# No token columns zeroed, a drain of GpSimd ahead of the last stores, other homes for a tile and two banks, and weight splits and choosing tied to later steps

## The chip, the cores and the metric

The kernel runs on one core of one Trainium2 chip. The metric is device time in microseconds. Three runs of the kernel before took 411.88, 405.08 and 408.65 us; their median is 408.65.

## The reference

Two layers follow each other. The first is a linear attention with a decay per channel, over B=4 batches, H=8 heads, S=768 steps and D=48 channels. The second is a mixture of experts over the N = 3072 tokens that come out, with DM = 384 channels, E = 8 experts, F = 1024 hidden units and room for 768 tokens in each expert.

```python
f = 1.0 / (1.0 + np.exp(-f_logit))
for t in range(S):
    state = f[:, :, t, :, None] * state + np.einsum('bhd,bhe->bhde', k[:, :, t], v[:, :, t])
    y[:, :, t] = np.einsum('bhd,bhde->bhe', q[:, :, t], state)
x = y.transpose(0, 2, 1, 3).reshape(B * S, H * D)

logits = x @ w_gate
expert_idx = np.argmax(logits, axis=1)
gate_w = softmax(logits)[np.arange(N), expert_idx]
# disp[e] holds the tokens of expert e in their order, at most 768 of them
h = np.maximum(np.einsum('ecd,edf->ecf', disp, w1), 0.0)
y = np.einsum('ecf,efd->ecd', h, w2)
out[i] = gate_w[i] * y[expert_idx[i], pos[i]]      # of the tokens that had room
```

## The kernel before, in words

**Attention.** The 3072 steps of all batches are cut into NT = 24 chunks of 128. A chunk is worked on over several slots of a loop that runs from slot -4 to slot 24 and is written out in order for all engines. Slot n finishes the output of chunk n-1 (`y_out`, ScalarE), pads queries and keys of chunk n+3 (POOL), transposes those of chunk n+2 on TensorE (PE, L343) and multiplies them by the decay's running products on DVE into kT and qT (L388, the products from two scans at L363 and L377), makes the scores of chunk n+1 (PE L399, evicted by ACT L405, masked by POOL L407), and then, for chunk n itself, the part from the carried state (L440), the keys' transposes (L424), the state's update by keys and values (L451) and the values (L481).

**Loads of attention.** SP issues them one after another, each some chunks ahead: `load("v", n + 3)` and `load("kq", n + 6)` in slot n, six buffers for v (ld_v) and three for kq (L195 is kq's load). In slots 1 and 3 SP also zeroes 256 rows of `disp` each (`zero_disp`), and in slots 2 to 5 the token column of 128 rows for each of seven experts (`zero_tokens`, L324). `disp` is the table in memory to which the tokens are sorted by expert, 393 numbers a row: 384 of x, eight logits and the token's number. A row that isn't filled is to hold zero as token, so that its output is dropped. Both read a tile `zero` of zeros (L314), which lies in the pool `apool`, whose memory later tiles reuse.

**Routing.** The rows of a chunk (PE L502) get their logits and are copied to a buffer. Groups of chunks (6, 6, 3, 3, 3, 1, 1, 1) are then routed together: `choose` (DVE, L533 to L540) makes the one-hot choice r_oh from the logits, for a single chunk `choose_one` (its last operation is L552); `rank` counts on PE how many earlier tokens went to each expert (L581, L582, L585, L588); `place` (DVE, L558 to L570) makes row numbers `ri`; and POOL scatters the rows into `disp` by an indirect DMA (L297), one per chunk, 24 in all. A group is chosen in the slot after its last chunk's rows and ranked in the slot after that; for groups that end in the last six chunks both happen in one slot.

**Weights.** Each weight matrix is split into a high and a low part of a narrower type (L131 on ACT for the high one, L140 on DVE or POOL for the low one), and each product is three matmuls: high by high, high by low, low by high. w1 comes in three raw pieces, w2 in four. Expert 0's pieces are loaded and split during attention, in the slots of `PIECE_LOAD` and `PIECE_SPLIT`.

**The experts.** The first 256 tokens of expert 0 are job 0. The first layer of that job runs inside the last slots of attention, by the table `EARLY`: `early_pe(ft)` is the product of hidden block ft (L662, nine matmuls), `early_out(ft)` its eviction into hh (ACT, L668) and hl (DVE, L669). Then attention's accumulators in PSUM, the pools psF and psY (two banks each), are closed and psM (four banks) takes their place. Job 0's second layer (L881) starts; in its middle `order_experts` sorts the seven other experts by their numbers of tokens, and `fill_rows` (three indirect stores of `zero` on POOL) clears the rows of each that its job's size takes in beyond its tokens. Job 1 is expert 0's remaining 224 tokens, and the seven others follow with sizes 480, 440, 424, 408, 396, 384 and 368. Each job loads its rows (`load_rows`), splits and transposes them (`prep`, L1023), computes its gate from the logits in the row (`gates`, L854 is its first difference from the maximum), runs the first layer (`ffn1`, eight hidden blocks of nine matmuls each) and the second, either by rows (`ffn2_rows`, L881, eviction L885) or by channels (`ffn2`, L1049, eviction yT L1054, transposed back at L1065). The output rows go to memory by indirect stores of POOL, 30 in all. For jobs from the third on, the next expert's seven pieces are loaded and split while the present job runs (`load_weights`), through three raw buffers; w1's low parts are made by DVE, w2's by POOL.

**The order.** Attention is written out by hand for all engines, job 0's second layer for PE alone. Everything else is ordered by the scheduler of the language, which runs the program on its own model of durations. `tc.issue_after(ins)` holds an instruction back behind another in that order.

## Time and profile before

| what | value |
|---|---|
| median of three runs | 408.65 us |
| profiled execution, its own time | 409.31 us |
| its span | 407.6 us |
| mean granted clock of TensorE | 0.984 |
| PE busy | 380.5 us, 93% |
| DVE busy | 214.4 us, 53% |
| ACT busy | 208.5 us, 51% |
| POOL busy | 174.6 us, 43% |
| mean DMA rate | 149 GB/s |

Attention takes roughly the first 155 us of the span, job 0's second layer the next few, and the jobs up to 398 us; the rest is the last stores and the program's end. A row of the chain of waits gives the instruction's start in us, its length, the engine or queue, the line with its operation, and in brackets how long the engine had been idle before it and what ended that. SPq, ACTq and POOLq are the engines' own queues with their register, issuing and drain instructions, which do not count as busy. L1285 is the end of the program, where each engine drains.

### The profile page before, as it was taken

How to read it: one execution, taken by the hardware profiler on the slowest of the kernel's cores; microseconds unless marked ns; L12 is line 12 of the kernel's file. 1: busy time of each engine (PE TensorE's matmuls, PEld its weight loads, DVE VectorE, ACT ScalarE, POOL GpSimd, SP SyncE). 2: the span in 40 equal slices, each digit the busy share in tenths (PEclk: the TensorE clock that was granted, in tenths of full speed). 3: DMA queues.
4: the chain of work that ended last, by engine and by line, in shares of the span. 5: the costliest groups of instructions: out<-in, count | busy, mean ns of one | idle time of the engine just before them, and what ended most of it. 6: DMA issues, size and time to landing. Idle time of an engine off the chain costs nothing.

```text
span 407.6 us, 10048 instructions
## 1 busy us (share of the span) xinstructions
PE 380.5 (93%) x3941; PEld 351.3 (86%) x3941; DVE 214.4 (53%) x502; ACT 208.5 (51%) x449; POOL 174.6 (43%) x233
## 2 busy tenths in 40 slices
PE   7699999989899898979999999999999999999990
PEld 7588888877788787979879989999999999999990
DVE  4987897858898654555635262253153262231300
ACT  3467677757677751255546453563563564432210
POOL 7444446757668431408163804424424415421010
PEclk9999999989999998999999999999999999999996
DMA  9999989999994221557676744425525323001010
GB/s 164 185 167 195 192 148 259 239 191 252 251 231 121 80 81 47 200 183 222 241 235 224 242 139 151 168 86 166 170 92 168 124 96 100 39 16 52 0 42 18
DMA packets 86957, 60.91 MB, mean 149 GB/s; under 512 B 69303, under 2 KB 81461, under 8 KB 86900
## 3 DMA queue, kind: packets, MB, share of 16 engines
q1 hardware_dynamic: 82852, 50.05, 51.5%
q0 software_dynamic: 3520, 9.92, 6.7%
q8 instruction: 33, 0.54, 0.6%
q10 hardware_dynamic: 528, 0.20, 0.2%
q14 instruction: 24, 0.20, 0.2%
HBM read 49.42 MB, written 11.44 MB: 149 GB/s over the span
## 4 chain that ended last, share of the span: by engine, by line
PE 53%; issue 15%; DVE 10%; DMA 10%; SPq 3%; ACT 3%; POOL 3%; POOLq 0%; ACTq 0%; DVEq 0%
PE psM L1049 14%; PE psA L662 7%; PE psM L662 7%; DMA ld_v<-in_v_dram 5%; PE psM L881 5%; PE psT L502 4%; DVE Rq L377 4%; PE psA L399 3%; DMA raw<-in_moe_w_dram 3%; SPq L195 2%; POOL out_dram L297 2%; PE psT L1022 2%; PE psT L424 2%; PE psY L440 2%; PE psF L662 2%
## 5 line engine op out<-in xcount | busy, mean ns | idle before, releaser
L140 POOL TENSOR_TENSOR w2l<-raw,w2h 128x768 fp32r<-128x768 f32 x28 | 51.4, 1844 | 78.8 <-ACT w2h L131 66.2
L297 POOL DMA_INDIRECT out_dram<-yo,g_ti x30 | 29.4, 981 | 74.1 <-ACT yo L885 43.5
L669 DVE SCALAR_TENSOR_TENSOR hl<-psA,hh 128x224 fp32r<-128x224 f32 (+7 forms) x32 | 17.9, 563 | 60.6 <-ACT hh L668 60.6
L131 ACT ACTIVATE w2h<-raw 128x768 fp32r<-128x768 f32 x32 | 27.1, 846 | 28.9 <-PE psM L1049 15.4
L407 POOL TENSOR_SCALAR_AFFINE_SELECT AT<-AT 128x512 f32<-128x512 f32 x48 | 29.3, 634 | 28.1 <-ACT AT L405 28.1
L881 PE MATMUL psM<-w2h,hh 128*128 128x384 f32 (+2 forms) x112 | 38.7, 348 | 1.6 <-DVE g_m L854 0.9
L881 PE MATMUL psM<-w2h,hl 128*128 128x384 f32 (+2 forms) x112 | 38.2, 344 | 0.2 <-DVE hl L669 0.2
L881 PE MATMUL psM<-w2l,hh 128*128 128x384 f32 (+2 forms) x112 | 38.2, 344 | 0.0
L1049 PE MATMUL psM<-hh,w2h 128*128 128x440 f32 (+3 forms) x96 | 34.3, 357 | 0.0
L405 ACT ACTIVATE AT<-psA 128x512 f32<-128x512 f32 x48 | 26.0, 594 | 16.0 <-PE psA L399 16.0
L1049 PE MATMUL psM<-hh,w2l 128*128 128x440 f32 (+3 forms) x96 | 33.9, 353 | 0.0
L1049 PE MATMUL psM<-hl,w2h 128*128 128x440 f32 (+3 forms) x96 | 33.8, 352 | 0.0
L669 DVE SCALAR_TENSOR_TENSOR hl<-psM,hh 128x224 fp32r<-128x224 f32 (+7 forms) x32 | 17.8, 563 | 28.3 <-ACT hh L668 28.3
L297 POOL DMA_INDIRECT disp<-rows,ri x24 | 25.6, 1066 | 16.0 <-DVE hl L669 5.2
L668 ACT ACTIVATE hh<-psA 128x224 fp32r<-128x224 f32 (+7 forms) x32 | 15.8, 498 | 30.7 <-PE psA L662 25.5
L363 DVE TENSOR_TENSOR_SCAN Suf<-psF,direv 112x511 f32<-112x511 f32 x24 | 29.1, 1211 | 4.4 <-PE psF L343 4.4
L382 POOL COPY kqp<-ld_kq 128x768 f32<-128x768 f32 x24 | 19.9, 830 | 24.2 <-DMA ld_kq<-in_q_dram 19.3
L662 PE MATMUL psM<-xh,w1h 128*128 128x480 f32 (+6 forms) x84 | 29.8, 355 | 0.0
L662 PE MATMUL psM<-xl,w1h 128*128 128x480 f32 (+6 forms) x84 | 29.7, 354 | 0.0
L140 DVE TENSOR_TENSOR w1l<-raw,w1h 128x1024 fp32r<-128x1024 f32 x21 | 24.8, 1222 | 9.1 <-ACT w1h L131 8.8
L399 PE MATMUL psA<-qT,kT 48*128 48x128 f32 x384 | 29.0, 280 | 0.4 <-DVE r_sel L558 0.2
L662 PE MATMUL psA<-xh,w1h 128*128 128x480 f32 (+6 forms) x84 | 29.4, 350 | 0.0
(223 smaller groups left out, 976.4 us busy)
## 6 DMA issues: line engine op xcount, KB each, us to landing
raw<-in_moe_w_dram SPq DMA_DIRECT2D x24, 512.0 KB, 7.2
raw<-in_moe_w_dram SPq DMA_DIRECT2D x32, 384.0 KB, 3.8
ld_kq<-in_k_dram SPq DMA_DIRECT2D x24, 192.0 KB, 6.6
ld_kq<-in_q_dram SPq DMA_DIRECT2D x24, 192.0 KB, 5.6
ld_v<-in_v_dram SPq DMA_DIRECT2D x24, 192.0 KB
ld_f<-in_f_logit_dram SPq DMA_DIRECT2D x11, 384.0 KB, 6.4
xg<-disp SPq DMA_DIRECT2D x6, 589.5 KB, 5.3
xg<-disp SPq DMA_DIRECT2D x3, 393.0 KB, 3.1
```

The costliest lines, as they stand in the source:

```text
L131: nc.scalar.activation(hi, raw, AF.Copy)
L140: engine.tensor_tensor(lo[cs], raw[cs], hi[cs].bitcast(F32), op=ALU.subtract)
L297: ins = nc.gpsimd.indirect_dma_start(out=dst, out_offset=bass.IndirectOffsetOnAxis(ap=idx, axis=0), in_=rows, in_offset=None, bounds_check ...
L363: nc.vector.tensor_tensor_scan(out=_view(Suf[:R], m - 1, [[-1, m]]), data0=_view(F, m, [[-1, m]]), data1=_view(direv[:R], m - 1, [[-1, m]] ...
L382: nc.gpsimd.tensor_copy(kqp[n % 2][:, :, :, :D], loaded("kq", n).rearrange("t h j d -> t j h d"))
L399: nc.tensor.matmul(pas[s][:, p], kTs[n][r, p], qTs[n][r, p], start=True, stop=True)
L405: nc.scalar.activation(AT[:, s], pas[s], AF.Copy)
L407: nc.gpsimd.affine_select(AT[:, s], AT[:, s], pattern=[[0, NP], [1, C]], compare_op=ALU.is_ge, fill=0.0, base=0, channel_multiplier=-1)
L662: nc.tensor.matmul(ph[:, :T], a[:, c, fs], x[:, c, :T], start=(n == 0), stop=(n == 3 * DT - 1))
L669: nc.vector.scalar_tensor_tensor(out=hl[:, :T], in0=ph[:, :T], scalar=0.0, in1=hh[:, :T].bitcast(F32), op0=ALU.max, op1=ALU.subtract)
L881: nc.tensor.matmul(py[:n], x[:, ks], a[:, ft], start=(ft == 0 and m == 0), stop=(ft == FT - 1 and m == 2))
L1049: nc.tensor.matmul(pys[c][:, :T], a[:, ft, cs], x[:, :T], start=(ft == 0 and n == 0), stop=(ft == FT - 1 and n == 2))
```

## The change

Eight edits are made together.

- `zero_tokens` and its four stores are gone. In `gates` the row number made from the token is taken to be at least zero (`tensor_scalar_max`), one more DVE operation in each of the nine gate calculations. The rows up to each job's size are still cleared by `fill_rows` as before.
- The tile `zero` lies in the pool `const`, which is kept to the end of the program.
- The pool psY is made ahead of psF, so that psM's first two banks are those that were psY's.
- The last block of the early job, `early_pe(7)`, moves behind the last chunk's rows.
- Where a group of several chunks ends before the last six chunks, `choose` waits for the next slot and stands there behind `kq_in`, that is behind the next kT and qT. Four groups are concerned.
- The low parts of expert 0's w2 pieces (DVE) move behind the routing of their slot.
- `load_weights` loads and splits only w1's three pieces. Each of w2's four pieces has its load and split called behind one of the last four hidden blocks of the present job, and the split held behind that block's hh. The first sorted job's own weights are still loaded as before.
- `gpsimd.drain()` is issued behind the last output store of the job before the last, ahead of the last job's three stores.

```diff
@@ -79,8 +79,8 @@
     psT = ctx.enter_context(tc.tile_pool(name="psT", bufs=2, space=PSUM))
     psA = ctx.enter_context(tc.tile_pool(name="psA", bufs=2, space=PSUM))
     pctx = ExitStack()
+    psY = pctx.enter_context(tc.tile_pool(name="psY", bufs=2, space=PSUM))
     psF = pctx.enter_context(tc.tile_pool(name="psF", bufs=2, space=PSUM))
-    psY = pctx.enter_context(tc.tile_pool(name="psY", bufs=2, space=PSUM))
 
 
     ident = const.tile([P, P], F32, name="ident")
@@ -128,7 +128,7 @@
 
     def split_high(piece):
         raw, hi, lo = piece
-        nc.scalar.activation(hi, raw, AF.Copy)
+        return nc.scalar.activation(hi, raw, AF.Copy)
 
     def split_low(piece, engine, parts=1):
         raw, hi, lo = piece
@@ -144,8 +144,13 @@
         split_low(piece, engine)
 
     def load_weights(wt, e, pool):
-        for n in range(DT + FT // 2):
-            split_piece(weight_piece(wt, e, pool, n), nc.vector if n < DT else nc.gpsimd)
+        for n in range(DT):
+            split_piece(weight_piece(wt, e, pool, n), nc.vector)
+
+    def load_later(wt, e, pool, n, ins):
+        piece = weight_piece(wt, e, pool, n)
+        with tc.issue_after(ins):
+            split_piece(piece, nc.gpsimd)
 
     wsets = [weight_tiles(w0pool)]
     xg0 = w0pool.tile([P, T_FIRST[0] // P, W], F32, name="xg0")
@@ -309,7 +314,7 @@
         return ins.ins
 
 
-    zero = apool.tile([P, W], F32, name="zero")
+    zero = const.tile([P, W], F32, name="zero")
     pace = {}
     nc.vector.memset(zero, 0.0)
 
@@ -317,12 +322,6 @@
         ins = nc.sync.dma_start(
             disp[v * RPE : v * RPE + 2 * P, :].rearrange("(a p) w -> p a w", p=P),
             zero.unsqueeze(1).broadcast_to([P, 2, W]),
-        )
-        after(ins, pace["ins"], "behind the first loads")
-
-    def zero_tokens(a):
-        ins = nc.sync.dma_start(
-            dispv[1:NE, a * P : (a + 1) * P, W - 1 :].rearrange("v p o -> p v o"), zero[:, :NS].unsqueeze(2)
         )
         after(ins, pace["ins"], "behind the first loads")
 
@@ -646,7 +645,8 @@
         (NT - 1, 1): ((early_out, 3), (early_pe, 4)),
         (NT - 1, 2): ((early_out, 4), (early_pe, 5)),
         (NT, 0): ((early_out, 5), (early_pe, 6)),
-        (NT, 1): ((early_out, 6), (early_pe, 7)),
+        (NT, 1): ((early_out, 6),),
+        (NT, 2): ((early_pe, 7),),
     }
 
     def early_job(n, at):
@@ -665,13 +665,13 @@
     def hidden_out(ph, T, ft, pool, size):
         hh = pool.tile([P, size], F32R, name=f"hh{ft}")
         hl = pool.tile([P, size], F32R, name=f"hl{ft}")
-        nc.scalar.activation(hh[:, :T], ph[:, :T], AF.Relu)
+        ins = nc.scalar.activation(hh[:, :T], ph[:, :T], AF.Relu).ins
         nc.vector.scalar_tensor_tensor(
             out=hl[:, :T], in0=ph[:, :T], scalar=0.0, in1=hh[:, :T].bitcast(F32), op0=ALU.max, op1=ALU.subtract
         )
-        return hh, hl
-
-    pieces, checks, chosen, split_at = {}, [], {}, {"n": None}
+        return hh, hl, ins
+
+    pieces, checks, chosen, split_at, full = {}, [], {}, {"n": None}, []
     slots = range(-4, NT + 1)
     ends = {g + m - 1: (g, m) for g, m in GROUPS}
 
@@ -703,8 +703,6 @@
                 load("f", 4)
         if n in (1, 3):
             zero_disp(0 if n == 1 else NE)
-        if 2 <= n < 6:
-            zero_tokens(n - 2)
         if n in PIECE_LOAD:
             k = PIECE_LOAD.index(n)
             pieces[k] = weight_piece(wsets[0], 0, raw0, k)
@@ -729,6 +727,9 @@
             kq_pad(n + 3)
         if kqn:
             kq_in(n + 2)
+        while full:
+            g, m = full.pop()
+            chosen[g] = choose(rows_of[g // RT][:, g % RT : g % RT + m], m, abuf), m
         if n == -2:
             keep_busy(7)
         if n % 2 and fn and n not in (-3, 1):
@@ -779,12 +780,12 @@
             queue.extend(range(g, g + m))
             if g + m == SPLIT:
                 split_at["n"] = n + 1
-        for k in pieces:
-            if PIECE_SPLIT[k] == n:
-                split_low(pieces[k], nc.vector)
         if prev and done and not tail:
             g, m = done
-            chosen[g] = choose(rows_of[g // RT][:, g % RT : g % RT + m], m, abuf), m
+            if n - 1 >= NT - 2 * NCH:
+                chosen[g] = choose(rows_of[g // RT][:, g % RT : g % RT + m], m, abuf), m
+            else:
+                full.append(done)
         if cur:
             values(n)
         if n % 2 == 0 and n and fn:
@@ -812,6 +813,9 @@
                 flush_scatter()
         else:
             early_job(n, 2)
+        for k in pieces:
+            if PIECE_SPLIT[k] == n:
+                split_low(pieces[k], nc.vector)
         if n == 4:
             nc.gpsimd.tensor_copy(cap, cap_i[:, 0:1])
         if n == NT - 5:
@@ -866,7 +870,10 @@
         nc.vector.reciprocal(out=gate, in_=gate)
         ti = fpool.tile([P, nb], I32, name="g_ti", bufs=4)
         nc.vector.tensor_scalar_add(ti, xg[:, :, W - 1], float(TOK0))
+        nc.vector.tensor_scalar_max(ti, ti, 0.0)
         return gate, ti
+
+    out_ins = []
 
     def ffn2_rows(wt, hs, pr, T, fpool, hooks=None):
         w1h, w1l, w2h, w2l = wt
@@ -876,14 +883,14 @@
             ks = slice(kb * P, kb * P + n)
             py = psM.tile([P, DM], F32, name="psM")
             for ft in range(FT):
-                hh, hl = hs[ft]
+                hh, hl = hs[ft][:2]
                 for m, (x, a) in enumerate(((hh, w2h), (hl, w2h), (hh, w2l))):
                     nc.tensor.matmul(py[:n], x[:, ks], a[:, ft], start=(ft == 0 and m == 0), stop=(ft == FT - 1 and m == 2))
                 if hooks and (kb, ft) in hooks:
                     hooks[kb, ft]()
             yo = fpool.tile([P, DM], F32, name="yo", bufs=2 if hooks else 3)
             nc.scalar.activation(yo[:n], py[:n], AF.Copy, scale=gate[:n, kb : kb + 1])
-            scatter(out, ti[:n, kb : kb + 1], yo[:n], N - 1, ("out",))
+            out_ins.append(scatter(out, ti[:n, kb : kb + 1], yo[:n], N - 1, ("out",)))
 
     with tc.manual_schedule(
         engines={
@@ -1026,7 +1033,7 @@
             gate, ti = gates(xg, nb, fpool)
         return xh, xl, gate, ti
 
-    def ffn1(wt, pr, T, hook, pools):
+    def ffn1(wt, pr, T, hook, later, pools):
         xh, xl, gate, ti = pr
         hs = []
         for ft in range(FT):
@@ -1036,13 +1043,15 @@
             hs.append(hidden_out(ph, T, ft, hpool, TMAX))
             if ft == 2 and hook is not None:
                 hook()
+            if ft >= FT // 2 and later is not None:
+                later(DT + ft - FT // 2, hs[ft][2])
         return hs
 
     def ffn2(wt, hs, T):
         w1h, w1l, w2h, w2l = wt
         pys = [psM.tile([P, TMAX], F32, name="psM") for _ in range(DT)]
         for ft in range(FT):
-            hh, hl = hs[ft]
+            hh, hl = hs[ft][:2]
             for c in range(DT):
                 cs = slice(c * P, (c + 1) * P)
                 for n, (a, x) in enumerate(((w2h, hh), (w2h, hl), (w2l, hh))):
@@ -1091,9 +1100,15 @@
         if j + 2 < len(jobs):
             with tc.issue_after(raws[-1]):
                 xgs[j + 2] = load_rows(expert(j + 2), jobs[j + 2][1])
+        later = None
         if 1 < j < len(jobs) - 1:
-            load_weights(wsets[jobs[j + 1][2]], expert(j + 1), rawpool)
-        hs = ffn1(wsets[ws], pr, T, hook, ((psA, "psA"), (psM, "psM")))
+            into, e = wsets[jobs[j + 1][2]], expert(j + 1)
+            load_weights(into, e, rawpool)
+            later = lambda n, ins, into=into, e=e: load_later(into, e, rawpool, n, ins)
+        if j == len(jobs) - 1:
+            with tc.issue_after(out_ins[-1]):
+                nc.gpsimd.drain()
+        hs = ffn1(wsets[ws], pr, T, hook, later, ((psA, "psA"), (psM, "psM")))
         cur = pr
         if j + 1 < len(jobs):
             pr = prep(xgs.pop(j + 1), jobs[j + 1][1])
```

On PE at the end of attention, the instructions read before as follows. psF and psT are the accumulators of `early_pe`, L502 is the last chunk's rows, L581 to L588 its ranking, L881 the start of job 0's second layer.

```order
L662 MATMUL psF<-x0h,w1h 128x256
L662 MATMUL psF<-x0l,w1h 128x256
L662 MATMUL psF<-x0h,w1l 128x256
L502 MATMUL psT<-identc,yT 64x104 x8
L581 LDWEIGHTS onesb
L581 MATMUL psA<-base_195,onesb 128x8
L582 LDWEIGHTS onesb
L582 MATMUL psA<-ohc,onesb 128x8
L588 LDWEIGHTS tri
L588 MATMUL psA<-r_oh,tri 128x8
L881 MATMUL psM<-w2h,hh_2951 128x384
```

Now the same place reads as below, where the line numbers are those of the changed kernel (L501 for L502, L580 to L587 for L581 to L588, L888 for L881).

```order
L501 MATMUL psT<-identc,yT 64x104 x8
L662 MATMUL psF<-x0h,w1h 128x256
L662 MATMUL psF<-x0l,w1h 128x256
L662 MATMUL psF<-x0h,w1l 128x256
...
L580 LDWEIGHTS onesb
L580 MATMUL psA<-base_195,onesb 128x8
L581 LDWEIGHTS onesb
L581 MATMUL psA<-ohc,onesb 128x8
L587 LDWEIGHTS tri
L587 MATMUL psA<-r_oh,tri 128x8
L888 MATMUL psM<-w2h,hh_2947 128x384
```

The nine matmuls of the last hidden block, which stood ahead of the rows, now stand between the rows and the ranking.

On DVE in a slot after a group of three chunks is complete, the order before was the choice (L533 to L540), then kT and qT, then the next scan.

```order
L533 TENSOR_REDUCE r_m<-rows 128x3
L535 TENSOR_TENSOR r_w<-rows,r_m 128x24
L536 TENSOR_TENSOR r_w<-r_w,desc 128x24
L538 TENSOR_REDUCE r_wm<-r_w 128x3
L540 TENSOR_TENSOR r_oh<-r_w,r_wm 128x24
L388 TENSOR_TENSOR kT<-psT,Suf_140 112x512
L388 TENSOR_TENSOR qT<-psT,Rq 112x512
L363 SCALAR_TENSOR_TENSOR Suf_142<-psF,direv 112x511
```

In the changed kernel (L532 to L539 for the choice, L387 for kT and qT, L362 for the scan) it is this.

```order
L387 TENSOR_TENSOR kT<-psT,Suf_140 112x512
L387 TENSOR_TENSOR qT<-psT,Rq 112x512
L532 TENSOR_REDUCE r_m<-rows 128x3
L534 TENSOR_TENSOR r_w<-rows,r_m 128x24
L535 TENSOR_TENSOR r_w<-r_w,desc 128x24
L537 TENSOR_REDUCE r_wm<-r_w 128x3
L539 TENSOR_TENSOR r_oh<-r_w,r_wm 128x24
L362 SCALAR_TENSOR_TENSOR Suf_142<-psF,direv 112x511
```

The five operations of the choice have changed places with kT and qT.

On ACT from the later hidden blocks of the job of 440 rows to the next job, before: hh are the evictions of hidden blocks, w1h and w2h the high parts of the next expert's weights, xh the next job's rows, yT this job's second layer.

```order
L668 ACTIVATE hh_4111<-psA 128x440
L131 ACTIVATE w1h<-raw 128x1024 x3
L668 ACTIVATE hh_4125<-psM 128x440
L1023 ACTIVATE xh<-psT 128x424 x2
L131 ACTIVATE w2h<-raw 128x768 x2
L1023 ACTIVATE xh<-psT 128x424
L859 ACTIVATE g_sp<-g_d 128x32
L860 ACTIVATE g_sn<-g_d 128x32
L131 ACTIVATE w2h<-raw 128x768
L1054 ACTIVATE yT<-psM 128x440 x2
```

Now the stretch reads as follows (L1030 for xh, L1063 for yT, L863 and L864 for the gate).

```order
L668 ACTIVATE hh_4103<-psA 128x440
L131 ACTIVATE w2h<-raw 128x768
L668 ACTIVATE hh_4121<-psM 128x440
L1030 ACTIVATE xh<-psT 128x424
L131 ACTIVATE w2h<-raw 128x768
L1030 ACTIVATE xh<-psT 128x424
L131 ACTIVATE w1h<-raw 128x1024 x2
L1030 ACTIVATE xh<-psT 128x424
L131 ACTIVATE w1h<-raw 128x1024
L863 ACTIVATE g_sp<-g_d 128x32
L864 ACTIVATE g_sn<-g_d 128x32
L1063 ACTIVATE yT<-psM 128x440 x3
```

w2's splits have moved up between the last hidden blocks, and w1's splits, by now those of the expert after the next, stand between the rows of the next job and ahead of yT.

## What the change is predicted to do, and why

> **What bounds the kernel now.** I read the page first (shares, slices), then who TensorE (PE) waited for, then the stretches round its gaps.
>
> ```profile
> span 407.6 us, 10048 instructions
> PE 380.5 (93%) x3941; PEld 351.3 (86%) x3941; DVE 214.4 (53%) x502; ACT 208.5 (51%) x449; POOL 174.6 (43%) x233
> ```
>
> PE is the bound almost everywhere; what can be won is its gaps, the stretches in which its clock is not full, and the end, where it has nothing to do. The next answer cuts the span there; the columns are busy time and number for PE, PEld, DVE, ACT and POOL, then the granted clock, the DMA share and GB/s.
>
> ```profile
> 79.90:83.30 3.40, 1.52 (x20) 1.14 (x20) 2.07 (x5) 2.08 (x5) 1.98 (x3) 1.00 0.81 165
> 83.30:86.80 3.50, 3.34 (x48) 3.04 (x50) 2.35 (x6) 2.00 (x7) 1.53 (x3) 0.56 1.19 207
> 86.80:90.20 3.40, 3.40 (x74) 3.07 (x72) 2.90 (x7) 2.14 (x4) 0.88 (x2) 0.95 1.04 171
> 155.00:158.40 3.40, 1.40 (x21) 0.90 (x21) 1.83 (x12) 0.77 (x2) 0.13 (x1) 1.00 0.16 59
> 158.40:162.00 3.60, 3.58 (x12) 3.35 (x12) 1.16 (x7) 0.32 (x2) 0.97 (x1) 0.56 0.17 60
> 162.00:165.40 3.40, 3.40 (x20) 3.34 (x20) 2.76 (x19) 0.58 (x1) 0.00 (x0) 0.96 0.35 118
> 213.00:398.00 185.00, 184.73 (x1038) 178.59 (x1035) 61.59 (x128) 82.12 (x149) 62.83 (x48) 1.00 0.34 116
> 398.00:407.60 9.60, 0.00 (x0) 0.00 (x0) 0.00 (x0) 0.39 (x1) 0.96 (x1) 0.67 0.07 19
> ```
>
> Twice a stretch with PE under half busy (1.52 of 3.40, 1.40 of 3.40) is followed by one at clock 0.56. From 213 to 398 PE is full, so nothing is to be had there and only something to lose. The last 9.6 us have no PE work. The gaps themselves, with who ended them in brackets:
>
> ```profile
> 83.46 0.73 PE L451 MATMUL psA<-ld_v,kn 128*64 128x48 f32 x15 [1.95 <-DMA ld_v<-in_v_dram]
> 106.77 0.41 PE L424 MATMUL psT<-ident,kT 112*128 112x112 f32 x2 [1.04 <-DVE kT L388]
> 138.12 0.19 PE L585 MATMUL psA<-r_oh,onesb 128*128 128x16 bf16 x2 [1.25 <-DVE r_oh L540]
> 157.30 0.17 PE L588 MATMUL psA<-r_oh,tri 128*128 128x8 bf16 x1 [1.07 <-DVE r_oh L552]
> 158.42 0.42 PE L881 MATMUL psM<-w2h,hh 128*128 128x384 f32 x1 [0.95 <-DVE g_m L854]
> 177.51 0.37 PE L662 MATMUL psA<-x0h,w1h 128*128 128x224 f32 x1 [2.07 <-DVE hl L669]
> 210.30 0.45 PE L881 MATMUL psM<-w2h,hh 128*128 128x384 f32 x1 [0.64 <-ACT hh L668]
> 210.99 0.44 PE L881 MATMUL psM<-w2h,hl 128*128 128x384 f32 x1 [0.24 <-DVE hl L669]
> ```
>
> **The change part by part.** The sum is made against the profiled execution: 409.3 us, of which the span is 407.6.
>
> A, the token columns. Four small stores leave SP's queue.
>
> ```profile
> L324 SPq DMA_DIRECT2D disp<-zero x4: 1095/1348/1608, 36.7 to 53.9; - x4
> 53.94 1.61 SPq L324 DMA_DIRECT2D disp<-zero  x1
> 55.67 2.38 SPq L195 DMA_DIRECT2D ld_kq<-in_k_dram  x1
> 75.48 7.84 DMA ld_v<-in_v_dram
> ```
>
> They occupy SP for about 4 x 1.35 = 5.4 us, and SP goes from one issue to the next without rest (53.94 + 1.61 = 55.55, next at 55.67). The load that PE lacked at 83.46 is issued by that queue at 75.48, 7.84 us before it lands in the chain. If SP's time is what holds the loads back, it comes 5.4 us sooner; if the DMA engines do (share 0.8 to 1.2 here), by less, down to almost nothing, since the stores are 4 x 7 x 128 = 3,584 packets of four bytes. It must come 1.95 us sooner for the gap to close; between 0 and 5.4 I take that it does, because the time lies nearer to what four issues cost. Then the clock stays full: 48 PE instructions took 3.5 us at 0.56, and by the next stretch's 74 in 3.4 us they take 2.2, so 1.2 more (an estimate; other work is mixed in). A = 1.95 + 1.2 = 3.1, bounds 0 and 3.2. The next values loads then need to come as much earlier; they follow on the same queue, which is also earlier.
>
> The page "TensorE: Matmul & The Clock Gate" of the Trainium skill, in Part 1 on the clock gate, has PE fall to half rate after a whole idle window of about 3.4 us. By that rule neither gap here would lower the clock, and A and C would be 2.7 smaller together; the trace disagrees, with PE 1.4 to 1.5 us busy in the stretch before each drop.
>
> B, DVE's order in attention. The choice of experts (five small operations) moves behind the next kT and qT, and w2's low half behind the routing.
>
> ```profile
> 104.47 1.01 DVE r_w L535
> 106.11 0.61 DVE kT L388
> 136.25 0.87 DVE w2l L140
> ```
>
> At 106.77 PE waited for a kT that stood behind the choice, so 1.04 goes; but PE's ranking now comes after a choice that starts about 1.2 us later (behind kT and qT, L388), and waits for r_oh instead: I count 0.2. The 0.87 of w2l stood before the choice that PE awaited at 138.12: 0.9 goes. B = 1.1, bounds -1 and 2.
>
> C, the end of attention. The last early_pe group moves behind the last rows_pe, and psM begins on psY's banks.
>
> ```profile
> 154.15 1.08 PE psF L662 x9
> 157.94 0.34 DVE hl L669
> ```
>
> Rows, choice and ranking all come 1.1 earlier, and the nine matmuls fill the 1.07 in which PE waited for r_oh. PE then waited until 158.42 because psM's first bank was psF's, whose last reader was hl at 157.94 to 158.28; psY's was read long before. So the second layer starts at 157.30 - 1.1 + 0.2 = 156.4 instead of 158.42: 2.0. With 12 matmuls in 3.6 us at clock 0.56 against 20 in 3.4 at 0.96, the cold stretch costs 3.6 - 12 x 0.17 = 1.5. C = 3.5, bounds 1 and 3.7. What is late next is the load of the second expert's rows, whose scatter comes only 1.1 earlier; it should land as PE arrives, give or take half a microsecond.
>
> D, the zero tile. Its old place is under hh of the second job, so ACT waited for the fill stores that read it.
>
> ```profile
> 169.89 6.60 DMA disp<-zero,fill_at
> 176.67 0.36 ACT L668 ACTIVATE hh<-psA 128x224 fp32r<-128x224 f32 x1 [5.18 <-DMA disp<-zero,fill_at]
> ```
>
> With the tile in const this wait goes and PE's 2.07 with it. D = 2.1, bounds 0 and 2.1; the rows for the third job follow the fill by 3.5 us of earlier start and then come just in time.
>
> E, weights. At 210 PE lacked hh, because in ACT's queue hh stood behind a split whose raw piece had not landed.
>
> ```profile
> 207.94 0.85 ACT L131 ACTIVATE w2h<-raw 128x768 fp32r<-128x768 f32 x1 [3.40 <-DMA raw<-in_moe_w_dram]
> ```
>
> Now w2's splits are tied behind the fifth to eighth hh, and w1's loads come a phase sooner. E = 0.9, bounds -1 and 0.9. The added maximum is one more small DVE operation in each of nine gate calculations; DVE is busy 62 of 185 us there, so 0.
>
> F, the drain. Each engine drains at the end, ACT in a moment, POOL not:
>
> ```profile
> L1285 POOLq DRAIN  x3: 44/107/4796, 402.0 to 407.3; - x3
> L1285 ACTq DRAIN  x2: 8/44/81, 401.6 to 407.0; - x2
> L1274 POOLq DRAIN  x1: 188/188/188, 0.4 to 0.4; - x1
> 391.12 0.97 POOL L297 DMA_INDIRECT out_dram<-yo,g_ti  x1 [16.17 <-ACT yo L885]
> ```
>
> At the start of the kernel, before any indirect store, POOL's drain takes 0.19 us; after 57 of them (24 of attention's rows, 3 fills, 30 of the output) it takes 4.80. If it counts the stores since the last drain, one that stands before the last three leaves 0.1 + 4.7 x 3/57 = 0.35. It lies itself in a hole of 16.17 us on POOL, with only the last three stores queued behind it, so it costs nothing; without that cover it would delay them by its 4.8. F = 4.4, bounds 0 and 4.6; I take 4.4, as three drains of one run give 0.04 to 0.19 with nothing new behind them.
>
> The page "VectorE: DVE Perf Modes" of the Trainium skill, under the drain one can't avoid, calls the drains of preamble and postamble a constant 12 ns or so on all five engines. By it F would be 0 and the sum 4.4 less; the trace agrees for ACT (0.08 us at most) and not for POOL.
>
> Sum: 3.1 + 1.1 + 3.5 + 2.1 + 0.9 + 4.4 = 15.1, so 409.3 - 15.1 = 394.2. The median of 408.65 lies 0.7 lower; against that I set about 1 for the two loads that come just in time. Forecast 394.5.
>
> **The rivals.** The drain is a fixed price of any indirect store: then three stores before the end cost as much as 57, F is 0 and the time 398.9. For it: only three drains were seen late, all at the end. Chance 0.2.
>
> The loads of attention stay behind: four-byte stores were never what held SP, the DMA engines were, and the gap at 83 stays or moves. A is 0, the time 397.6; for it the DMA share of 1.19. Chance 0.13. With the first rival too: 402.
>
> Slower: ACT's queue in the sorted jobs. w1's splits for the job after next now stand ahead of the yT evictions and must wait for pieces that can only be loaded once w2's pieces, tied to late hh's, have freed the three raw buffers.
>
> ```profile
> raw<-in_moe_w_dram SPq DMA_DIRECT2D x24, 512.0 KB, 7.2
> raw<-in_moe_w_dram SPq DMA_DIRECT2D x32, 384.0 KB, 3.8
> L140 POOL TENSOR_TENSOR w2l<-raw,w2h 128x768 fp32r<-128x768 f32 x28 | 51.4, 1844 | 78.8 <-ACT w2h L131 66.2
> 258.14 1.74 PE psM L662 x9
> 249.59 6.82 PE psM L1049 x33
> 241.04 8.03 PE psM L1049 x39
> ```
>
> From the fifth hh the chain is split 2.7 (w2h 0.85, w2l 1.84), load 3.8, split 2.7, load 7.2, w1h 0.85 x 1024/768 = 1.1: 17.5 us. PE takes three groups of 1.74 and 15.4 of second layer (241.04 to 256.41): 20.6. So there is a margin of 3 us in each of five jobs. It decides if a piece lands in over 10 us instead of 7.2; at 15 us each job loses 15 - 10.2 = 4.8, five of them 24, and the time is 418. Against it: DMA share 0.34 there. Chance 0.05; a milder form, in which a few microseconds are lost (400 to 408), 0.12.
>
> **How the numbers follow.** All six parts near their size: 0.5, at 391 to 397.5. Drain 0.2, loads 0.13, lost in part 0.12, slower 0.05. The range must leave out no more than 2 in 10: from 389.5 (all upper bounds, 409.3 - 16.5 = 392.8, less the 3.4 by which the runs scatter) to 402 (drain and loads both). A measurement here tells about 2% from no change, that is below 400.5 and above 416.8. Faster: 0.5 + 0.2 + 0.1 = 0.8, the loads' case with some of its weight lost to both failing; within 2%: 0.16; slower: 0.04, most of the slow case.
>
> **What would show it.** No PE wait for ld_v near 80 and the clock full from start to end (A, C); the second layer of the first job 1 us behind the last ranking's release at most (C); hh of the second job with no DMA as its releaser (D); a POOLq DRAIN of several us before the last three stores and none over 0.5 at the end (F); 213 to 398 as full as now, shifted by 10 to 11 us (E). It is wrong if PE shows new gaps behind yT or hh in the sorted jobs, or if the last drain is still 4.8.

## The result, and the profile after

The changed kernel took 394.8 us (median of four runs, 393.5 to 399.62), the kernel before 407.86 us beside it (405.08 to 411.88); the ratio is 0.9691 with a 95% interval of 0.9616 to 0.9767. Six more runs in another session gave 394.93 us and 0.9624 (0.9577 to 0.9672). The forecast was 394.5 us. One of the changed kernel's first four runs, the one of 399.62 us, had a lower granted clock (0.986) and is left out of the ratio.

The page of the changed kernel, its span, its busy times and the clock that was granted in 40 slices:

```profile
span 391.4 us, 10037 instructions
PE 376.8 (96%) x3941; PEld 348.4 (89%) x3941; DVE 214.8 (55%) x511; ACT 208.9 (53%) x449; POOL 174.9 (45%) x233
PEclk9999999999999999999999999999999999999999
```

The span is 16.2 us shorter, and the clock is at 90% or more in every slice. The stretches in which it stood low before, and the two long ones behind them, now read as follows (busy time and number for PE, PEld, DVE, ACT and POOL, granted clock, DMA share, GB/s):

```profile
80.00:90.00 10.00, 9.75 (x203) 8.62 (x203) 8.68 (x24) 7.87 (x21) 7.30 (x12) 1.00 0.87 197
156.00:160.00 4.00, 4.00 (x25) 4.00 (x24) 2.94 (x21) 0.58 (x1) 1.47 (x2) 1.00 0.43 150
160.00:165.00 5.00, 5.00 (x44) 4.92 (x43) 2.47 (x12) 1.95 (x6) 3.49 (x5) 1.00 0.90 303
213.00:380.00 167.00, 167.00 (x938) 161.79 (x937) 56.85 (x120) 76.44 (x138) 57.19 (x43) 1.00 0.35 113
380.00:391.40 11.40, 6.03 (x35) 5.67 (x33) 0.00 (x0) 1.16 (x2) 2.33 (x3) 0.97 0.15 51
```

From 213 to 380 us PE is busy without a gap. What it still waits for in the whole kernel, in its larger rows (line waited for: total us, times, longest; two rows of the first 13 us are left out):

```profile
PE psF L342 <- DVE Rq L376: 1.7, 6, 0.6
...
PE psA L584 <- DVE r_oh L539: 0.9, 2, 0.5
PE psM L888 <- DVE hl L669: 0.9, 1, 0.9
```

Waits for ld_v, for the fill stores' hh and for hh behind a split are gone from the list. The drains, on POOL's queue: L1110 is the new one, L1300 the program's end.

```profile
L1110 POOLq DRAIN  x1: 5707/5707/5707, 362.0 to 362.0; - x1
L1300 POOLq DRAIN  x3: 50/107/360, 390.2 to 391.1; - x3
362.28 0.98 POOL L302 DMA_INDIRECT out_dram<-yo,g_ti  x1 [3.19 <-ACT yo L892]
386.97 0.96 POOL L302 DMA_INDIRECT out_dram<-yo,g_ti  x1 [3.24 <-ACTq L1273]
```

The last drain takes 0.36 us instead of 4.80. From the last store's start to the end of the span there are 391.4 - 386.97 = 4.4 us, where there were 407.6 - 398.67 = 8.9.

Where the time went is best seen in milestones: the starts of the same matmuls in PE's timelines of the two profiles.

| milestone | before | after | gained so far |
|---|---|---|---|
| rows of the 3rd chunk | 34.60 | 33.81 | 0.8 |
| rows of the 12th chunk | 80.57 | 79.87 | 0.7 |
| rows of the 13th chunk | 89.81 | 85.87 | 3.9 |
| rows of the 21st chunk | 134.28 | 129.97 | 4.3 |
| rows of the 22nd chunk | 143.19 | 138.01 | 5.2 |
| rows of the last chunk | 155.16 | 148.90 | 6.3 |
| second layer of job 0 | 158.42 | 152.07 | 6.35 |
| second layer of job 1 | 178.61 | 168.37 | 10.2 |
| second layer of the job of 480 | 206.23 | 196.01 | 10.2 |
| second layer of the job of 440 | 240.97 | 229.34 | 11.6 |
| end of the last matmul | 397.73 | 386.03 | 11.7 |
| end of the span | 407.6 | 391.4 | 16.2 |

The 0.8 us at the top was won before the first of the stores that are now left out was issued (36.7 us in the profile before), and the prediction has no term for it. It goes with the place of the zero tile, as the section on that tile shows.

### The profile page after: what moved, and what is told of

It reads as the page before. It is cut to its first block, busy times and chain, and to the rows that moved or that the text cites. A ratio compares the mean times of both kernels' runs of the same rounds, so it can differ in the third digit from the quotient of the medians.

```text
span 391.4 us, 10037 instructions
## 1 busy us (share of the span) xinstructions
PE 376.8 (96%) x3941; PEld 348.4 (89%) x3941; DVE 214.8 (55%) x511; ACT 208.9 (53%) x449; POOL 174.9 (45%) x233
## 4 chain that ended last, share of the span: by engine, by line
PE 71%; issue 9%; DVE 8%; ACT 3%; SPq 3%; POOL 2%; DMA 2%; POOLq 1%; DVEq 0%; ACTq 0%
PE psM L1058 14%; PE psA L662 12%; PE psM L662 11%; PE psM L888 9%; PE psT L501 5%; DVE Rq L376 5%; PE psA L398 4%; PE psY L439 2%; PE psT L423 2%; PE psT L1029 2%; ACT rows L513 2%; PE psF L662 2%; SPq L200 2%; PE psF L342 2%; DMA ld_kq<-in_q_dram 2%
## 5 line engine op out<-in xcount | busy, mean ns | idle before, releaser
L140 POOL TENSOR_TENSOR w2l<-raw,w2h 128x768 fp32r<-128x768 f32 x28 | 51.1, 1852 | 39.1 <-ACT w2h L131 39.1
L406 POOL TENSOR_SCALAR_AFFINE_SELECT AT<-AT 128x512 f32<-128x512 f32 x48 | 29.3, 634 | 36.4 <-ACT AT L404 36.3
L131 ACT ACTIVATE w1h<-raw 128x1024 fp32r<-128x1024 f32 x24 | 25.2, 1059 | 25.5 <-DMA raw<-in_moe_w_dram 25.5
L888 PE MATMUL psM<-w2h,hh 128*128 128x384 f32 (+2 forms) x112 | 37.8, 342 | 0.9 <-DVE hl L669 0.9
L888 PE MATMUL psM<-w2l,hh 128*128 128x384 f32 (+2 forms) x112 | 37.8, 339 | 0.0
L888 PE MATMUL psM<-w2h,hl 128*128 128x384 f32 (+2 forms) x112 | 37.6, 337 | 0.0
L1058 PE MATMUL psM<-hh,w2l 128*128 128x440 f32 (+3 forms) x96 | 33.8, 352 | 0.0
L362 DVE TENSOR_TENSOR_SCAN Suf<-psF,direv 112x511 f32<-112x511 f32 x24 | 29.0, 1210 | 4.4 <-PE psF L342 4.4
```

The lines of the kernel that those rows point to most:

```text
L131: return nc.scalar.activation(hi, raw, AF.Copy)
L140: engine.tensor_tensor(lo[cs], raw[cs], hi[cs].bitcast(F32), op=ALU.subtract)
L362: nc.vector.tensor_tensor_scan(out=_view(Suf[:R], m - 1, [[-1, m]]), data0=_view(F, m, [[-1, m]]), data1=_view(direv[:R], m - 1, [[-1, m]] ...
L406: nc.gpsimd.affine_select(AT[:, s], AT[:, s], pattern=[[0, NP], [1, C]], compare_op=ALU.is_ge, fill=0.0, base=0, channel_multiplier=-1)
L888: nc.tensor.matmul(py[:n], x[:, ks], a[:, ft], start=(ft == 0 and m == 0), stop=(ft == FT - 1 and m == 2))
L1058: nc.tensor.matmul(pys[c][:, :T], a[:, ft, cs], x[:, :T], start=(ft == 0 and n == 0), stop=(ft == FT - 1 and n == 2))
```

## The experiments

In some executions, in 4 of the 14 profiles, PE's clock is at half between 14 and 23 us, which costs 3 to 5 us, and it does so in kernels like the one before and in kernels like the changed one; so kernels are compared below by how far their milestones shift after the 3rd chunk, and not by their spans.

### The token columns, left out, issued elsewhere, and made smaller

The first kernel is the one before without the four stores (and with the clamp of the row number):

```diff
-        if 2 <= n < 6:
-            zero_tokens(n - 2)
```

> The kernel before with the first edit alone: no token columns zeroed, the row number clamped in the gates. If SP's time for the four stores (5.4 us) held the loads back, TensorE's wait of 1.95 us for ld_v near 83 us is gone, the clock stays at 1.00 there, and everything behind it comes about 3.1 us earlier than in the kernel before (span near 404.5). If the gain there came from another edit, the wait and the dip of the clock are still there and the span stays near 407.6.

Measured: span 402.6, and 3.2 us gained between the rows of the 12th and the 13th chunk (0.6 behind the kernel before, then 2.6 ahead of it). The wait at 83 us is gone and the clock is full there, as the theory had it. PE comes there 0.6 us later than in the kernel before, which by itself could hide no more than 0.6 of the wait's 1.95.

The second issues the same stores from ACT's queue:

```diff
-        ins = nc.sync.dma_start(
+        ins = nc.scalar.dma_start(
             dispv[1:NE, a * P : (a + 1) * P, W - 1 :].rearrange("v p o -> p v o"), zero[:, :NS].unsqueeze(2)
```

> The kernel before with the same four token stores, issued from ScalarE's queue instead of SP's. Theory (SP's issuing time is what mattered): the wait for ld_v near 83 us is gone as without the stores, 3 us gained, less what ScalarE loses by four issues of 1.1 to 1.6 us. Rival (the 3,584 packets of four bytes slow the transfers themselves, whoever issues them): a wait of about 2 us for a load stays, and with it the dip of the clock; nothing gained.

Measured: span 411.9. ACT came to a stand for 8 us at the first store, and PE with it. The first row is from PE's waits, the others from ACT's timeline.

```profile
PE psA L451 <- ACT kn L429: 7.6, 1, 7.6
...
27.46 1.09 ACT L405 ACTIVATE AT<-psA 128x512 f32<-128x512 f32 x2
36.02 0.48 ACTq L324 DMA_DIRECT2D disp<-zero  x1
36.55 0.54 ACT L429 ACTIVATE kn<-psT 128x448 f32<-128x448 f32 x1 [8.01 <-DMA ld_kq<-in_k_dram]
```

The wait for ld_v was gone, but the loads had been given 8.7 us by PE's own delay, so this tells nothing of the two theories, and what the store waited for isn't settled. The drain's experiment below warns of the same: there the stores are still made, PE is 3.6 us late from the start, and the wait for ld_v is gone too (3.6 behind becomes 0.4 behind at the 13th chunk). The gap was a close race between loads and PE, and a delay of PE that is longer than the gap hides it.

The third leaves the issues in SP's queue and takes six sevenths of the packets away; at another place it also makes psY ahead of psF:

```diff
-            dispv[1:NE, a * P : (a + 1) * P, W - 1 :].rearrange("v p o -> p v o"), zero[:, :NS].unsqueeze(2)
+            dispv[1:2, a * P : (a + 1) * P, W - 1 :].rearrange("v p o -> p v o"), zero[:, :1].unsqueeze(2)
...
+    psY = pctx.enter_context(tc.tile_pool(name="psY", bufs=2, space=PSUM))
     psF = pctx.enter_context(tc.tile_pool(name="psF", bufs=2, space=PSUM))
-    psY = pctx.enter_context(tc.tile_pool(name="psY", bufs=2, space=PSUM))
```

> The kernel before with two edits at different places. First, the four token stores are issued as before but write the token column of one expert instead of seven (512 packets of four bytes instead of 3,584; the zeroing of the other six experts' columns is left out). If the number of issues in SP's queue holds the loads back, most of the wait for ld_v near 83 us stays (over 1 us) and the clock dips; if the packets do, it is gone as without the stores. Second, psY is made ahead of psF, with everything else of job 0 as before. By the forecast's term C the second layer of job 0 would start about 0.9 us sooner after the last ranking than before (1.12 us after its matmul's start); by the theory that psM waits for both closed pools, nothing moves there.

Measured, with the four issues, the stretch round 85 us, and the start of job 0's second layer:

```profile
L324 SPq DMA_DIRECT2D disp<-zero x4: 930/1109/1852, 37.1 to 52.0; - x4
...
80.00:90.00 10.00, 9.73 (x198) 8.37 (x196) 8.70 (x21) 7.57 (x20) 7.31 (x13) 1.00 1.05 193
...
154.30 0.17 PE L588 MATMUL psA<-r_oh,tri 128*128 128x8 bf16 x1 [1.07 <-DVE r_oh L552]
155.42 0.66 PE L881 MATMUL psM<-w2h,hh 128*128 128x384 f32 x1 [0.95 <-DVE g_m L854]
```

The issues still take SP 0.9 to 1.9 us each, some 5 us together. Yet the gap is gone and the same 3.2 us are gained (0.4 behind, then 2.8 ahead). So SP's 5 us of issuing don't make the gap without the packets; that the packets would make it without SP's time isn't shown, as the stores from ACT's queue could not tell. This run also starts 0.4 us late against the kernel before, again much less than the gap. And the swap of the pools does nothing by itself: 155.42 - 154.30 = 1.12 us, as before.

### The drain, alone and earlier

The kernel before with the drain alone:

```diff
+        if j == len(jobs) - 1:
+            with tc.issue_after(out_ins[-1]):
+                nc.gpsimd.drain()
         hs = ffn1(wsets[ws], pr, T, hook, ((psA, "psA"), (psM, "psM")))
```

> The kernel before with the drain alone, behind the last store of the job before the last. Theory (the drain's price counts the indirect stores since the drain before): a drain of about 5 us in the hole of 16 us, the one at the end 0.3 to 0.4 instead of 4.80, the span 4.4 shorter (403.2), and nothing else moved. Rival (a fixed price of any indirect store, or the short last drain of the changed kernel came from another edit): 4.8 at the end again, span 407.6.

Then the changed kernel with its drain two jobs earlier, behind the last store of the job of 408:

```diff
-        if j == len(jobs) - 1:
-            with tc.issue_after(out_ins[-1]):
-                nc.gpsimd.drain()
...
                 hook()
+                if T == T_SORTED[-3]:
+                    with tc.issue_after(out_ins[-1]):
+                        nc.gpsimd.drain()
```

> The changed kernel with its drain moved two jobs forward, so that ten indirect stores lie behind it instead of three. If the price counts stores, at 4.8 / 57 = 0.084 us each, the last drain takes 0.1 + 10 x 0.084 = 0.9 to 1.0 us and the drain in the middle 47/54 of the 5.7 of the changed kernel, 5.0 (it reads longer than its price, since it lies over the store before it). Rival (one drain anywhere late is enough, its price having to do with the kernel's beginning): the last drain stays at 0.36. Where the drain stands now, work may be queued behind it on GpSimd; the hole there is smaller, so up to 3 us may be lost in the middle.

Measured, first of the drain alone (the new drain, the last one, the store before the new drain), then of the early one:

```profile
L1100 POOLq DRAIN  x1: 5695/5695/5695, 376.7 to 376.7; - x1
L1290 POOLq DRAIN  x3: 50/107/360, 405.0 to 405.9; - x3
376.98 0.97 POOL L297 DMA_INDIRECT out_dram<-yo,g_ti  x1 [3.19 <-ACT yo L887]
```

```profile
L1048 POOLq DRAIN  x1: 6913/6913/6913, 321.3 to 321.3; - x1
L1300 POOLq DRAIN  x3: 50/107/936, 394.4 to 395.9; - x3
323.37 0.90 POOL L302 DMA_INDIRECT out_dram<-yo,g_ti  x1 [0.30 <-ACT hh L668]
328.38 1.84 POOL L140 TENSOR_TENSOR w2l<-raw,w2h 128x768 fp32r<-128x768 f32 x1 [4.11 <-PE psM L1061]
```

A drain in the middle is put down from before the store ahead of it, so its own part is from that store's end: 382.40 - 377.95 = 4.45 us for 54 stores (362.0 + 5.71 - 363.26 = 4.45 in the changed kernel), 328.21 - 324.27 = 3.94 for 47. With the last drains there are five points: 3 stores 0.36, 10 stores 0.94, 47 stores 3.94, 54 stores 4.45, 57 stores 4.80. They lie on a line of 0.08 us per store since the drain before, and the fixed price and the price of the kernel's beginning are both out. The tail of the drain-alone kernel, from the last store at 401.67 to 406.2, is 4.5 us, about as in the changed kernel (4.4); its span is 406.2 and not 403.2 because this execution is 3.6 us late from the start. In the early place nothing was lost to the drain: the kernel's milestones stay 4.2 us behind the changed kernel's from the job of 480 to the last matmul, so the split that waits behind the drain (4.11 us idle) has slack.

### The zero tile back in its pool

```diff
-    zero = const.tile([P, W], F32, name="zero")
+    zero = apool.tile([P, W], F32, name="zero")
```

> The changed kernel with the tile zero back in its old pool. Theory: the first hh of the second job waits again for the fill stores, TensorE waits 2 us for it (two bounds: 1.5 and 4, since the job starts earlier against the fill than before), span 393.5 instead of 391.4. Rival (the earlier start or the other order freed that wait): no wait of ScalarE on a DMA there, span as the changed kernel.

Measured, PE's row and ACT's:

```profile
174.28 0.37 PE L662 MATMUL psA<-x0h,w1h 128*128 128x224 f32 x1 [2.15 <-DVE hl L669]
173.45 0.36 ACT L668 ACTIVATE hh<-psA 128x224 fp32r<-128x224 f32 x1 [5.26 <-DMA disp<-zero,fill_at]
```

The wait is back at 2.15 us. With what follows in its wake the second layer of job 1 is 2.8 us later than in the changed kernel (the 4.5 by which job 0's was already late taken off), the third job's 4.1. Part of the wake is the clock: it was granted at 0.79 and 0.78 in the two stretches of 4 us from 172.68 us on, where the changed kernel has 1.00 at the same place. The tile's place is what freed that time.

The same line also moves something at the start. The first row below is from the changed kernel, the second from this one; the last number is the rate of the DMA engines in GB/s.

```profile
10.00:12.00 2.00, 0.85 (x8) 0.66 (x6) 1.97 (x5) 0.00 (x0) 0.84 (x2) 1.00 1.32 226
10.00:12.00 2.00, 1.19 (x11) 1.00 (x9) 2.00 (x4) 0.00 (x0) 0.77 (x2) 1.00 1.39 177
```

The six profiles with the tile in apool have 172 to 179 GB/s in this stretch (the kernel before 174), the eight with it in const 216 to 234, whatever else differs. Near 20 us PE then waits for kqp, which POOL makes from a load: 0.45 to 1.00 us in the four profiles with the tile in apool and a full clock there, 0.29 in one of the six with it in const and a full clock, and not at all in the other five. That is where the changed kernel wins most of the 0.8 us at the top of the table of milestones. What it is worth by this line alone isn't shown, as this execution had its clock at half from 14 us on, and why the place of a tile changes the rate isn't shown either; the move also shifts the addresses of other tiles.

### The weights loaded as before

```diff
-        for n in range(DT):
-            split_piece(weight_piece(wt, e, pool, n), nc.vector)
+        for n in range(DT + FT // 2):
+            split_piece(weight_piece(wt, e, pool, n), nc.vector if n < DT else nc.gpsimd)
...
             load_weights(into, e, rawpool)
-            later = lambda n, ins, into=into, e=e: load_later(into, e, rawpool, n, ins)
```

> The changed kernel with the weights of the sorted jobs loaded and split as before. Theory: gaps of TensorE near 200 us, behind an hh that stands behind a split on ScalarE, 0.9 us as in the kernel before, up to 1.5 by the milestones of the two traces. Rival (the gaps had to do with the later start, not with the splits): no gap, same span.

Measured: 1.5 us lost between the second layers of job 1 and of the job of 480, and no more than 0.15 behind that. But the gap is not the old one at 210; it is another, at 193, and its row and the one on ACT that it hangs on are

```profile
193.21 0.49 PE L662 MATMUL psA<-xh,w1h 128*128 128x480 f32 x1 [0.99 <-DVE hl L669]
190.27 1.06 ACT L131 ACTIVATE w1h<-raw 128x1024 fp32r<-128x1024 f32 x1 [5.93 <-DMA raw<-in_moe_w_dram]
```

ACT waits for the raw piece of a w1, and the hh's of the job of 480 stand behind that split. The same gap is in kernels that keep the new loading (next but one and below). So the changed kernel was run again:

> The changed kernel once more, unaltered, to see what of the 1.5 us that its sorted jobs gained stays. In four kernels close to it TensorE waits 0.4 to 1.0 us near 193 us for an hh that stands on ScalarE behind a split of w1 whose raw piece has not landed. Theory now: that wait has to do with when the fill stores land, by chance 1.8 us sooner in the first profile of the changed kernel, not with the tied splits, so a wait of 0.4 to 1.0 us appears here too. Rival (the forecast's own reason, the tied splits): no wait between 165 and 262 us, as in the first profile. Time 393 to 400, by the clock in the first 20 us.

Measured, PE's row near 193 and the split:

```profile
192.25 0.49 PE L662 MATMUL psA<-xh,w1h 128*128 128x480 f32 x1 [0.25 <-DVE hl L669]
189.30 1.06 ACT L131 ACTIVATE w1h<-raw 128x1024 fp32r<-128x1024 f32 x1 [5.67 <-DMA raw<-in_moe_w_dram]
```

It is there, at 0.25 us, less than the 0.4 that was expected at least, and costs 0.6 us with its wake. In seven of the nine profiles of this family, in the table, the wait goes with how long after the start of job 0's second layer that first split begins. In the other two, with the early block (below) and with the tile put back, PE reaches this place some 2 and 4 us late by losses of their own; there it waits 0.35 us and not at all.

| kernel | split begins after | PE's wait near 193 |
|---|---|---|
| sorting hooked in earlier (below) | 35.4 | 0 |
| changed, first profile | 36.3 | 0 |
| changed, second profile | 37.0 | 0.25 |
| drain earlier | 37.4 | 0.58 |
| DVE's order as before | 37.7 | 0.94 |
| weights loaded as before | 37.9 | 0.99 |
| psM waits by tile (below) | 39.1 | 1.10 |

The kernel with the old loading lies on the same line as those with the new. From the start of job 0's second layer to that of the job of 440 the four with the new loading and otherwise the same FFN take 77.3, 77.9, 78.3 and 78.6 us, the old loading 78.8. That is 0.2 us above the slowest of the four and 1.5 above the fastest, so one run of the old loading can't say what the tied splits give, or whether they give anything. Nor does the gap at 210 need more than lateness to vanish: with the old loading put back the second layers of the jobs of 480 and 440 are 33.33 us apart, as in the changed kernel, and in the two profiles of kernels like the one before in which PE stood longest in job 1 (2.6 and 2.75 us) they are 33.3 and 33.6 apart, where the other three have 34.6 to 34.7.

### The last early block back in its place

```diff
-        (NT, 1): ((early_out, 6),),
-        (NT, 2): ((early_pe, 7),),
+        (NT, 1): ((early_out, 6), (early_pe, 7)),
```

> The changed kernel with the last early block back ahead of the last chunk's rows. Theory: TensorE waits again 1.07 us for r_oh, the second layer of the first job starts 1.1 us later (153.2 instead of 152.1), and since TensorE then stands still for 2 of 3.4 us as in the kernel before, the clock falls again and costs 1.5 more; 2.6 in all. Rival (the clock's fall needed something else of the kernel before): 1.1 alone.

Measured (the first two rows from PE's timeline, the third the stretch behind):

```profile
156.49 0.17 PE L587 MATMUL psA<-r_oh,tri 128*128 128x8 bf16 x1 [1.07 <-DVE r_oh L551]
157.60 0.66 PE L887 MATMUL psM<-w2h,hh 128*128 128x384 f32 x1 [0.95 <-DVE g_m L857]
157.60:161.00 3.40, 3.40 (x12) 3.40 (x12) 1.31 (x8) 0.32 (x2) 0.98 (x1) 0.55 0.18 64
```

The second layer starts 1.1 us later, the clock falls to 0.55, and by job 1's second layer 2.5 us are lost, as the theory said and not the rival. Another 1.6 are lost by the job of 480, of them 0.7 for the rows of the third job and 0.35 for an hh.

### DVE's order in attention as before

```diff
-        while full:
-            g, m = full.pop()
-            chosen[g] = choose(rows_of[g // RT][:, g % RT : g % RT + m], m, abuf), m
...
+        for k in pieces:
+            if PIECE_SPLIT[k] == n:
+                split_low(pieces[k], nc.vector)
         if prev and done and not tail:
             g, m = done
-            if n - 1 >= NT - 2 * NCH:
+            chosen[g] = choose(rows_of[g // RT][:, g % RT : g % RT + m], m, abuf), m
```

> The changed kernel with DVE's order in attention as before (choice ahead of kT and qT, w2's low parts ahead of the routing). Theory: the two waits come back, together 1.3 us, of it 0.4 net at the group near 103 us and 0.9 near 133. Rival (they had to do with the late loads of the kernel before): under 0.3.

Measured: 0.4 us lost near 103 us and 0.8 near 133, 1.2 in all, by the two waits of the kernel before:

```profile
PE psT L423 <- DVE kT L387: 1.3, 2, 1.0
PE psA L584 <- DVE r_oh L539: 1.3, 1, 1.3
PE psA L662 <- DVE hl L669: 0.9, 1, 0.9
```

The third row is the gap at 193 again, which took 1.3 us more here.

### What PE still waits for ahead of job 0's second layer

In the changed kernel this wait was not gone, though psM's first bank is now psY's:

```profile
151.04 0.17 PE L587 MATMUL psA<-r_oh,tri 128*128 128x8 bf16 x1
152.07 0.45 PE L888 MATMUL psM<-w2h,hh 128*128 128x384 f32 x1 [0.86 <-DVE hl L669]
```

The language lets a pool wait for what lay in its memory as a whole, or tile by tile; psM did the first.

```diff
-    psM = ctx.enter_context(tc.tile_pool(name="psM", bufs=4, space=PSUM))
+    psM = ctx.enter_context(tc.tile_pool(name="psM", bufs=4, space=PSUM, reuse_waits="tile"))
```

> The changed kernel with one option: psM waits tile by tile for what lay in its banks, instead of for the whole of the pools that were closed. Theory: the 0.86 us that TensorE still waits ahead of job 0's second layer is for the last reader of psF (hl), though psM's first bank was psY's; the wait goes and the second layer starts 0.8 us after the ranking's end sooner (ranking at 151.04, second layer at 151.1 to 151.3, in the first profile's times). Rival (TensorE needs hl or hh there for another reason): the wait stays at 0.86.

Measured:

```profile
150.82 0.17 PE L587 MATMUL psA<-r_oh,tri 128*128 128x8 bf16 x1
150.84 0.42 PE L888 MATMUL psM<-w2h,hh 128*128 128x384 f32 x1
173.56 0.52 PE L1029 MATMUL psT<-ident,xg 128*128 128x128 f32 x3 [0.37 <-DMA xg<-disp]
174.62 0.72 PE L1029 MATMUL psT<-ident,xg 96*128 96x96 f32 x5 [0.54 <-DMA xg<-disp]
192.90 0.49 PE L662 MATMUL psA<-xh,w1h 128*128 128x480 f32 x1 [1.10 <-DVE hl L669]
```

The wait is gone, the second layer starts 0.02 us behind the ranking instead of 1.03. And it is all lost again, and more: PE now comes too early for the third job's rows, which are loaded behind the fill stores, and the gap at 193 is at its longest. The span is 393.1. So the last kernel also starts the sorting of the experts sooner:

```diff
-                wsets[0], hs0, (None, None) + g0, T_FIRST[0], h0pool, {(0, 3): order_experts,
+                wsets[0], hs0, (None, None) + g0, T_FIRST[0], h0pool, {(0, 0): order_experts,
```

> The same option, and the sorting of the experts hooked in behind the first block of job 0's second layer instead of the fourth, so that the fill stores start 1.4 us sooner against the end of attention. Theory: both waits gone (0.86 ahead of the second layer, 0.4 to 1.0 near 193), nothing late next: 0.9 to 2 us under the changed kernel on the same chip. Rival (the rows of the third job wait for another thing than the fill): the wait near 193 stays, gain 0.9 at most.

Measured, the span, PE's start of the second layer and the split:

```profile
span 390.4 us, 10040 instructions
...
151.10 0.42 PE L888 MATMUL psM<-w2h,hh 128*128 128x384 f32 x1
186.47 1.06 ACT L131 ACTIVATE w1h<-raw 128x1024 fp32r<-128x1024 f32 x1 [3.78 <-DMA raw<-in_moe_w_dram]
```

PE has no gap from the last ranking to the end. Its last matmul ends at 385.03 us, 1.0 before that of the changed kernel's first profile and 1.85 before that of its second. Six times gave a median of 393.29 us against 394.93 in the same session; to the kernel before the ratio is 0.9632 (0.9583 to 0.9682), so by the times alone the two can't be told apart.

## Why the prediction was right, point by point

The sum was 15.1 us against the profiled execution, the spans differ by 16.2, and the profiled execution took 393.5 us where 394.2 was worked out. The terms, in the order of the prediction:

**A, the token columns: 3.1 forecast, 3.2 measured.** The size is right with both its parts, the wait and the clock. The reason given for taking the upper end failed: "the time lies nearer to what four issues cost". The run with small stores shows that fewer packets free the loads though SP still spends 5 us on four issues. The choice between the two ends came out well, by luck, for a reason that the prediction had put at the other end, and the rival of loads bound by the DMA engines was wrong in taking that to mean no gain: the small packets are themselves work for those engines. The page "DMA: Bandwidth & Descriptors" of the Trainium skill, under why small descriptors are slow, gives each packet a fixed cost whatever its size. That fits, though no run here measures the cost of one.

**B, DVE's order: 1.1 forecast, 1.3 measured** (0.4 and 0.9; 1.2 by undoing it). The first place was counted at 0.2 net, the wait of 1.04 less a new one for r_oh; the new one is 0.5 (the changed kernel's list of waits has r_oh with 0.9 us in two, the longest 0.5), and the place gave 0.4. The second gave its 0.9.

**C, the end of attention: 3.5 forecast, 2.5 to 2.9 measured.** The move of early_pe(7) gave its 1.1, and the clock 1.4 (by the run that undoes the move) to 1.8 (of the 3.9 us gained between the starts of the two second layers D has 2.07). The step that failed is "psM's first bank was psF's ... psY's was read long before": the banks never decided it, since a pool waits for all of the closed ones. The 0.86 us that stayed is that step's error, shown by the swap alone, which did nothing, and by the tile-wise wait, which took it away.

**D, the zero tile: 2.1 forecast, 2.07 by the row, 2.8 to 4.1 when undone in the changed kernel,** where the clock falls behind the wait. The 0.8 us at the start goes with the tile's place too; the prediction counted only the fill stores and put this at nothing.

**E, the weights: 0.9 forecast, 1.4 between the milestones, and not shown to be from the tied splits.** The step "in ACT's queue hh stood behind a split whose raw piece had not landed" describes the old gap well, but the same sentence holds for the new one at 193, which the change did not remove and which the first profile just escaped. Some 0.6 of the 16.2 us are that luck: in the second profile the last matmul ends at 386.88 against 386.03 us, 0.2 of it from the start.

**F, the drain: 4.4 forecast, 4.5 measured.** The count of stores, taken from one reading of 4.80 us and one of 0.19, is borne out by five points. The last drain was worked out as 0.35 and took 0.36. The page "VectorE: DVE Perf Modes" of the Trainium skill, under the drain one can't avoid, has the drains of the program's end at a constant 12 ns or so on all engines; POOL's last one takes 0.36 to 4.80 us in these runs.

**The rivals.** The fixed price of the drain fell to the 0.36; the slower rival, ACT's queue in the sorted jobs, did not come true: PE has no gap in the 167 us from 213 to 380. ACT's last w1 split and its first yT in the job of 440:

```profile
236.65 1.06 ACT L131 ACTIVATE w1h<-raw 128x1024 fp32r<-128x1024 f32 x1
...
243.60 1.74 ACT L1063 ACTIVATE yT<-psM 128x440 f32<-128x440 f32 x3 [3.71 <-PE psM L1058]
```

The split was done at 237.7 us, 5.9 before yT, where a margin of 3 was worked out. "About 1 for the two loads that come just in time" was set against the median: with PE 1.2 us earlier still, the third job's rows do make it wait, 0.37 and 0.54 us, so the load was indeed that close.

Against the profiles the sum was 1.1 us short: 0.8 from the start, for which it had no term, 0.5 in E, 0.4 in A, B and F together, less 0.6 or more too much in C. That the forecast lies 0.3 us from the median is better than its working: the profiled run happened to be the fastest of its four, 1.3 us under their median.

## What to carry to other kernels

When an engine has stood still behind a close race, undoing one edit, or merely being late from the start, makes the gap vanish or move; compare milestones on the timeline of the bound engine, and ask of each vanished gap whether the lateness hid it. A pool that takes over the memory of closed ones may wait for all of them, so changing which bank comes first does nothing until the wait is by tile. GpSimd's indirect stores leave a debt that its next drain pays, 0.08 us each here: a drain in a hole of that engine pays it where it costs nothing.

## What the runs showed of the hardware that I had not expected

The clock of PE at the kernel's start differs from run to run with the same instructions. The stretches are of the changed kernel and of the kernel with the drain alone, which are alike up to there in what PE does:

```profile
8.00:14.00 6.00, 4.17 (x69) 3.64 (x69) 5.93 (x12) 0.84 (x1) 1.90 (x8) 1.00 1.32 218
14.00:20.00 6.00, 5.41 (x104) 4.71 (x103) 5.75 (x9) 4.28 (x11) 3.40 (x6) 1.00 0.98 172
```

```profile
8.00:14.00 6.00, 3.80 (x54) 3.22 (x55) 5.93 (x11) 0.84 (x1) 1.94 (x7) 0.98 1.34 200
14.00:20.00 6.00, 6.00 (x65) 5.50 (x67) 4.78 (x8) 2.31 (x4) 2.87 (x4) 0.50 1.24 187
```

Four of the fourteen profiles have the second form and lose 3 to 5 us there (rows of the 3rd chunk at 37.1 to 38.5 us instead of 33.8 to 35.1, the kernel in which ACT stood still left out); that is as much as any one edit but the drain gave. PE is busy about two thirds of the stretch before, a little less in the four (3.80 to 3.95 of 6.0 us) than in the others (4.04 to 4.23). The page "TensorE: Matmul & The Clock Gate" of the Trainium skill, in Part 1, says that the window in which activity is watched runs freely, so that the same kernel can start differently from run to run; with that the profiles agree. It also wants a whole idle window of about 3.4 us for the fall to half rate; with that they don't, neither here, where PE's longest wait from 8 to 14 us was 1.1 us in the second profile, nor in the kernel with the early block back, where the longest wait before the clock fell to 0.55 was 1.07 us.
